# Adding the softmax sums' small constant on ScalarE instead of VectorE, in a newly drawn order of all steps

## The chip, the core and the metric

The kernel runs on one core of one Trainium2 chip. The metric is device time in microseconds (us) of one execution of the whole program. In the profile PE is TensorE, PEld its weight loads, DVE is VectorE, ACT is ScalarE, POOL is GpSimd, and SP is the engine that issues all transfers here.

## The reference

```
scores = scale * np.matmul(q, k.transpose(0, 1, 3, 2))        # 4 batches, 8 heads, 768 tokens, 64 wide
keep = is_sink | in_window                                    # 4 sink tokens, window of 128
scores = np.where(keep, scores, -1000000000.0)
scores = scores - np.max(scores, axis=-1, keepdims=True)
a = np.exp(scores)
a = a / (np.sum(a, axis=-1, keepdims=True) + 1e-09)
x = np.matmul(a, v)                                           # heads side by side: 3072 x 512
...
h = x @ w_in                                                  # 3072 x 1024
e = np.exp(h - h_max)
sm = e / (np.sum(e, axis=-1, keepdims=True) + 1e-09)
solu = h * sm
ln = (solu - mu) / np.sqrt(var + 1e-06) * g_ln
return ln @ w_out                                             # 3072 x 512
```

The change concerns the `+ 1e-09` in the attention's softmax.

## The kernel before

The 3072 tokens are worked in 24 chunks of 128 (chunk n, six for each batch). Since only 128 earlier keys and four sinks count, a chunk's scores need its own keys, those of the chunk ahead of it and the sinks. They lie in `ring`, where keys of four chunks fit.

The steps of one chunk, by the engine that does them:

- PE writes the scores of a head into one of two PSUM banks, `bank` (L654, L656, L657).
- DVE chooses between the two key chunks (`pick`, L663), adds the mask and takes the row's extreme (`mask`, L674, out `sc` and `nmx`). This frees the bank for the next but one head.
- ACT takes the exponential of each head and sums it (`exps`, L685, out `sc` and `ssum`).
- For four heads at a time (a half of the chunk, `hb`), DVE adds the constant to the 128x4 sums (L690, out `rs`) and inverts the result (L691). Both lines are the step `invert`; there are 48 of them.
- POOL multiplies the probabilities by the inverse: L700 in place, or L704 into `pn` for the chunks that are transposed by way of DRAM (`pd`, `pb`, then DVE L725). The others are transposed on PE (L732).
- POOL masks the transposed probabilities `pt` into `pc` and `pt` (L741, L747), and PE multiplies them with the values (`av`, L795).
- ACT and DVE split the result into a high part `xh` (L800) and a low part `xl` (L804), and PE multiplies both by the first weights (`h`, L815, three matmuls for each of eight pieces).
- Then come the row's maximum (DVE L820), the exponential (ACT L825), the product (DVE L830), the centring (ACT L846), a transposition by way of DRAM (`ud`, `ub`, DVE L872), the split into `uh` (ACT L886) and `ul` (DVE L890), and the second weights on PE (`o`, L902). ACT scales the result (L908), and SP stores it (L913).

At the start the weights come in as 64-bit words. They are narrowed by ACT and DVE (`wraw`, `wps`, `wbits`, lines 421 to 464), while the first chunks are already on their way. POOL also makes the low part of the keys (L625).

Nothing chooses the order at run time. The table `ORDER` at the head of the file lists all 2679 steps (a step is a function, a chunk and a part), and the program issues them in that order; each engine works its own instructions in the order in which they stand there, and waits for what is not ready:

```
    for at in ORDER:
        f, n, i = steps[at]
        f(n, i)
```

Of the kernel before, what the change touches and what calls it, by code (L numbers as in the profile page):

```python
# [157 lines left out]
P = 128  # L158
# [58 lines left out]
def _banded(ctx, tc, q, k, v, n_sink, window, w_in, w_out, g_ln, out, val, wts, wpool, consts):  # L217
# [11 lines left out]
    HB = 4  # L229
# [458 lines left out]
    def invert(n, hb):  # L688
        rs = st["rs", n, hb] = sm.tile([P, HB], F32, tag="rs", name=f"rs_{n}_{hb}")
        nc.vector.tensor_scalar(rs, st["ssum", n, hb], EPS_SUM, None, op0=ALU.add)  # L690
        nc.vector.reciprocal(rs, rs)  # L691
# [226 lines left out]
    def kept(k):  # L918
        return lambda n: 0 if carried(n) else k
# [201 lines left out]
```

## Time and profile before

| what | us |
|---|---|
| three runs | 438.46, 440.33, 1389.28 |
| their median | 440.33 |
| span of the profiled execution, first to last instruction | 437.9 |
| fastest run less that span | 0.56 |

The profile gives no other time for the profiled execution than its span. Busy times add an engine's instructions over the span, and a chain follows the work that ended last back to the start, at each step to what released it. Matmuls overlap each other in the records, so that PE's busy time holds short waits too.

### The profile page before, as it was taken

What the parts mean: (1) busy time and instruction counts of PE and PEld (TensorE: products, weight loads), DVE (VectorE), ACT (ScalarE), POOL (GpSimd) and SP (SyncE); (2) the same over time, 40 slices, a digit from 0 to 9 for tenths busy, and PEclk for the clock granted to TensorE, in tenths of its full rate; (3) what the DMA queues carried; (4) which work ended last, traced back from release to release, by engine and by line L of the source; (5) the groups of instructions that cost most, each with busy time, mean ns of one, the idle gap of its engine ahead of it and who ended that gap; (6) DMA issues with size and microseconds to landing.
All of it is one profiled execution on the core that took longest, in us unless ns stands there. A gap on an engine that the chain in (4) does not pass through costs nothing.

```text
span 437.9 us, 8516 instructions
## 1 busy us (share of the span) xinstructions
PE 415.4 (95%) x2507; PEld 332.6 (76%) x2507; DVE 360.9 (82%) x1029; ACT 315.7 (72%) x817; POOL 234.2 (53%) x388
## 2 busy tenths in 40 slices
PE   4899999999999999999999999999999999999994
PEld 3447777878787888878777787878878778888884
DVE  2989999997999889999989997899899797674520
ACT  5989988978877776877768576768767675555551
POOL 7742626658867552788454736556623673624020
PEclk9999999999999999999999999999999999999999
DMA  8999449999899899976998989966966558623001
GB/s 225 324 284 293 96 101 168 180 151 196 218 161 216 208 185 253 195 229 190 180 239 210 207 219 226 193 173 179 269 176 216 170 165 227 188 96 121 24 26 55
DMA packets 164025, 81.38 MB, mean 186 GB/s; under 512 B 120188, under 2 KB 150788, under 8 KB 163972
## 3 DMA queue, kind: packets, MB, share of 16 engines
q1 hardware_dynamic: 163972, 80.77, 82.3%
q8 instruction: 22, 0.36, 0.4%
q14 instruction: 31, 0.25, 0.2%
HBM read 45.62 MB, written 23.72 MB: 158 GB/s over the span
## 4 chain that ended last, share of the span: by engine, by line
PE 53%; DVE 25%; DMA 6%; issue 5%; POOL 4%; ACT 4%; SPq 1%; DVEq 0%; POOLq 0%; ACTq 0%
PE o L902 18%; PE h L815 17%; PE av L795 5%; DVE qT L600 4%; DVE sc L674 3%; DVE bank L663 3%; PE bank L656 3%; PE bank L657 2%; PE ws L443 2%; DMA pb<-pd 2%; DVE ul L890 2%; DVE nm L820 2%; PE bank L654 2%; DMA wraw<-in_moe_w_in_dram 1%; DVE pt L725 1%
## 5 line engine op out<-in xcount | busy, mean ns | idle before, releaser
L685 ACT ACTIVATE sc<-sc,nmx 128x132 f32<-128x132 f32 (+1 forms) x192 | 75.9, 396 | 25.1 <-DVE nmx L674 24.1
L902 PE MATMUL o<-w2h,uh 128*128 128x512 f32 (+1 forms) x200 | 79.7, 398 | 0.0
L815 PE MATMUL h<-w1h,xh 128*128 128x512 f32 x192 | 77.0, 401 | 1.0 <-DVE u L830 0.9
L902 PE MATMUL o<-w2h,ul 128*128 128x512 f32 (+1 forms) x200 | 77.0, 385 | 0.5 <-DVE ul L890 0.5
L902 PE MATMUL o<-w2l,uh 128*128 128x512 f32 (+1 forms) x200 | 77.2, 386 | 0.0
L815 PE MATMUL h<-w1h,xl 128*128 128x512 f32 x192 | 75.9, 395 | 0.6 <-DVE xl L804 0.5
L815 PE MATMUL h<-w1l,xh 128*128 128x512 f32 x192 | 75.3, 392 | 0.0
L625 POOL TENSOR_TENSOR ring<-kf,ring 64x512 fp32r<-64x512 f32 x48 | 63.1, 1320 | 22.6 <-ACT ring L620 18.7
L674 DVE CUSTOM_DVE_ANT_0 sc<-bank,bias 128x132 f32<-128x132 f32 (+1 forms) x192 | 53.1, 288 | 9.4 <-PE bank L654 1.7
L704 POOL TENSOR_TENSOR pn<-sc,rs 128x512 f32<-128x512 f32 x26 | 28.0, 1079 | 53.1 <-DVE rs L691 19.2
L656 PE MATMUL bank<-ring,qT 128*128 128x264 f32 (+1 forms) x176 | 51.0, 300 | 1.9 <-DVE nmx L674 1.7
L657 PE MATMUL bank<-ring,qX 128*128 128x264 f32 (+1 forms) x176 | 48.3, 284 | 0.1
L700 POOL TENSOR_TENSOR sc<-sc,rs 128x528 f32<-128x528 f32 (+1 forms) x22 | 24.8, 1127 | 40.8 <-DVE rs L691 24.0
L902 PEld LDWEIGHTS o<-w2h,ul 128*128 128x128 f32 x200 | 37.5, 188 | 9.2 <-DVE ul L890 1.2
L902 PEld LDWEIGHTS o<-w2h,uh 128*128 128x128 f32 x200 | 37.6, 188 | 8.8 <-issue 3.1
L741 POOL TENSOR_SCALAR_AFFINE_SELECT pc<-pt 128x512 f32<-128x512 f32 x40 | 28.4, 716 | 29.4 <-DVE pt L725 25.5
L815 PEld LDWEIGHTS h<-w1h,xl 128*128 128x128 f32 x192 | 36.0, 188 | 10.6 <-DVE xl L804 2.8
L656 PEld LDWEIGHTS bank<-ring,qT 128*128 128x128 f32 x176 | 33.1, 188 | 12.0 <-DVE nmx L674 6.3
L815 PEld LDWEIGHTS h<-w1h,xh 128*128 128x128 f32 x192 | 36.1, 188 | 7.3 <-issue 0.8
L902 PEld LDWEIGHTS o<-w2l,uh 128*128 128x128 f32 x200 | 37.7, 188 | 5.0
L825 ACT ACTIVATE e<-h,nm 128x1024 f32<-128x1024 f32 x24 | 26.7, 1113 | 18.7 <-DVE nm L820 18.6
L815 PEld LDWEIGHTS h<-w1l,xh 128*128 128x128 f32 x192 | 36.2, 188 | 5.0
(146 smaller groups left out, 975.9 us busy)
## 6 DMA issues: line engine op xcount, KB each, us to landing
qX<-qT SPq DMA_DIRECT2D x88, 128.0 KB, 2.7
ud<-u SPq DMA_DIRECT2D x20, 512.0 KB, 4.3
ub<-ud SPq DMA_DIRECT2D x80, 128.0 KB, 3.5
pd<-pn SPq DMA_DIRECT2D x26, 256.0 KB, 3.0
pb<-pd SPq DMA_DIRECT2D x52, 128.0 KB, 3.4
vn<-in_v_dram SPq DMA_DIRECT2D x24, 256.0 KB, 4.3
out_dram<-ob SPq DMA_DIRECT2D x23, 256.0 KB, 2.6
kn<-in_k_dram SPq DMA_DIRECT2D x12, 384.0 KB, 6.6
```

What stands on the lines that cost most here:

```text
L625: nc.gpsimd.tensor_tensor(t[ROWS[1 - x]], src[ROWS[x]], t[ROWS[x]].bitcast(F32), op=ALU.subtract)
L656: nc.tensor.matmul(o, st["qT", n, x][:, r, :], rhs, start=True, stop=False)
L657: nc.tensor.matmul(o, st["qX", n, x][:, r, :], rhs, start=False, stop=True)
L674: nc.vector.tensor_tensor_reduce(out=st["sc", n, hb][:, j, c0:c1], in0=st["s", n, h].rearrange("p a x -> p (a x)")[:, c0:c1], in1=bias0 if ...
L685: nc.scalar.activation(sc[:, i, c0:c1], sc[:, i, c0:c1], AF.Exp, bias=nmx[:, i:i + 1], scale=-1.0, accum_out=ssum[:, i:i + 1])
L700: nc.gpsimd.tensor_tensor(sc[:, :, c0:c1], sc[:, :, c0:c1], rs.unsqueeze(2).to_broadcast([P, HB, c1 - c0]), op=ALU.mult)
L704: nc.gpsimd.tensor_tensor(pn.rearrange("p g h f -> p h g f"), sc[:, :, 4:SEG].rearrange("p h (g f) -> p h g f", f=32), rs.unsqueeze(2).uns ...
L741: nc.gpsimd.affine_select(pc, st["pt", n, hb], pattern=[[0, HB], [1, P]], compare_op=ALU.is_ge, fill=0.0, base=0, channel_multiplier=-1)
L795: nc.tensor.matmul(acc[ROWS[x], r, :], vals[:, 2 * r + x, :], p[:, 2 * jp + x, :], start=alone, stop=alone or (r, i) == (NPAIR - 1, 1))
L815: nc.tensor.matmul(st["h", n][:, cols], a[:, kt, :], w[:, kt, cols], start=(kt == 0 and m == 0), stop=(kt == KT1 - 1 and m == 2))
L825: nc.scalar.activation(e, st["h", n], AF.Exp, bias=st["nm", n], scale=1.0, accum_out=se)
L902: nc.tensor.matmul(st["o", n, i], a[:, kt % 4, :], part(w, kt)[:, i * wide:(i + 1) * wide], start=(kt == 0 and m == 0), stop=(kt == KT2 - ...
```

## The change

The step `invert` keeps the reciprocal on DVE. The addition becomes a step of its own, `floor_sum`, in which ACT copies the 128x4 sums and adds the constant on the way. With 48 more steps the numbers of all steps shift, and the table `ORDER` is another one, with all steps in an order that was made anew. The tiles, the buffers, the transfers and the arithmetic are the same.

```
 ORDER = (
-    346, 0, 143, 2, 144, 244, 60, 348, 351, 5, 6, 3, 69, 350, 7, 51, 8, 352, 24, 9, 147, 154, 345, 12, 42, 155, 353,
...
 )
...
+    def floor_sum(n, hb):
+        rs = st["rs", n, hb] = sm.tile([P, HB], F32, tag="rs", name=f"rs_{n}_{hb}")
+        nc.scalar.activation(rs, st["ssum", n, hb], AF.Copy, bias=EPS_SUM)
+
     def invert(n, hb):
-        rs = st["rs", n, hb] = sm.tile([P, HB], F32, tag="rs", name=f"rs_{n}_{hb}")
-        nc.vector.tensor_scalar(rs, st["ssum", n, hb], EPS_SUM, None, op0=ALU.add)
+        rs = st["rs", n, hb]
         nc.vector.reciprocal(rs, rs)
...
-        rest_k: 2, ring_sinks: 1, score: H, pick: H, mask: H, exps: NPAIR, invert: NHB, normalise: NHB, turn_p: kept(NHB),
+        rest_k: 2, ring_sinks: 1, score: H, pick: H, mask: H, exps: NPAIR, floor_sum: NHB, invert: NHB, normalise: NHB, turn_p: kept(NHB),
```

What this does to an engine's instructions is seen at two places. In the changed file line numbers are 3 higher down to `exps` and 6 higher behind `invert`.

**First place: DVE at the first half of chunk 11**, with the low part `xl` of chunk 9 close by. Before, DVE has the addition, the reciprocal and then `xl`:

```order
L663 COPY_PREDICATED bank_89<-m_prev,bank_89 128x128
L674 ISA sc_1_2492,nmx_1_2493<-bank_89,bias_114 128x132
L674 ISA nmx_1_2493 128x1
L690 TENSOR_SCALAR rs_0_2507<-ssum_0_2414 128x4
L691 RECIPROCAL rs_0_2507<-rs_0_2507 128x4
L804 TENSOR_TENSOR xl_2511<-av_2432,xh_2486 128x512
L663 COPY_PREDICATED bank_90<-m_prev,bank_90 128x128
```

Now DVE has `xl` ahead of the reciprocal, and no addition:

```order
L810 TENSOR_TENSOR xl_2498<-av_2442,xh_2477 128x512
L666 COPY_PREDICATED bank_89<-m_prev,bank_89 128x128
L677 ISA sc_1_2494,nmx_1_2495<-bank_89,bias_114 128x132
L677 ISA nmx_1_2495 128x1
L666 COPY_PREDICATED bank_90<-m_prev,bank_90 128x128
L697 RECIPROCAL rs_0_2485<-rs_0_2485 128x4
L878 STREAM_TRANSPOSE ur_0_2511<-ub_2428 128x512
```

The addition of that half has gone to ACT, where it stands behind the last two exponentials of its half:

```order
L806 CAST xh_2477<-av_2442 128x512
L623 CAST ring<-kf_2238 64x4x128
L762 CAST sk_2380<-sc_1_2306 128x4x8
L688 ACTIVATE sc_0_2394,ssum_0_2396<-sc_0_2394,nmx_0_2395 128x132 x2
L693 ACTIVATE rs_0_2485<-ssum_0_2396 128x4
L688 ACTIVATE sc_1_2494,ssum_1_2496<-sc_1_2494,nmx_1_2495 128x132 x2
L892 CAST uh_0_2534<-ur_0_2511 128x512
```

So one DVE instruction of the half is gone, one ACT instruction has come, and `xl` stands one reciprocal and one head's mask earlier on DVE.

**Second place: PE between the values (`av`) and the first weights (`h`) of chunk 4.** Before, two pieces of chunk 1's second weights (`o`) and two heads' scores of chunk 5 (`bank`) stand between them:

```order
L795 MATMUL av_1242<-pt_1_1193,vn_629 64x128 x2
L902 MATMUL o_0_1269<-w2h_658,uh_0_1170 128x512
L902 MATMUL o_0_1269<-w2l_659,uh_0_1170 128x512
L902 MATMUL o_0_1269<-w2h_658,ul_0_1207 128x512
...
L656 MATMUL bank_89<-ring,qT_1_982 128x264
L657 MATMUL bank_89<-ring,qX_1_1015 128x264
L815 MATMUL h_1296<-w1h,xh_1289 128x512
```

Now five pieces of the second weights, four heads' scores and one transposition stand there:

```order
L801 MATMUL av_1254<-pt_1_1217,vn_672 64x128 x2
L659 MATMUL bank_90<-ring,qT_1_1012 128x264
L660 MATMUL bank_90<-ring,qX_1_1019 128x264
...
L908 MATMUL o_0_1276<-w2h_770,uh_0_1153 128x512
L908 MATMUL o_0_1276<-w2l_771,uh_0_1153 128x512
L908 MATMUL o_0_1276<-w2h_770,ul_0_1235 128x512
...
L738 MATMUL ptp_0_1311<-ident,sc_0_1100 128x128 x4
L908 MATMUL o_0_1276<-w2h_1085,uh_1_1290 128x512
L908 MATMUL o_0_1276<-w2l_1086,uh_1_1290 128x512
L908 MATMUL o_0_1276<-w2h_1085,ul_1_1305 128x512
L821 MATMUL h_1327<-w1h,xh_1322 128x512
```

So the first weights of that chunk stand three pieces, two heads' scores and a transposition further behind the values whose split they need. PE's work as a whole is the same.

## Rows read from the trace of the kernel before

**Rows 1.** The page's first part: busy us, share of the span and number of instructions of each engine.

```profile
PE 415.4 (95%) x2507; PEld 332.6 (76%) x2507; DVE 360.9 (82%) x1029; ACT 315.7 (72%) x817; POOL 234.2 (53%) x388
```

**Rows 2.** The page's chain of work that ended last, as shares of the span, by engine.

```profile
PE 53%; DVE 25%; DMA 6%; issue 5%; POOL 4%; ACT 4%; SPq 1%; DVEq 0%; POOLq 0%; ACTq 0%
```

**Rows 3.** Busy time in three stages of the span: from and to, length, then for PE, PEld, DVE, ACT and POOL busy us (instructions), the granted clock, DMA share and GB/s.

```profile
0.00:100.00 100.00, 88.70 (x508) 66.16 (x509) 85.82 (x253) 85.63 (x214) 54.42 (x93) 1.00 0.92 202
100.00:400.00 300.00, 294.42 (x1802) 239.08 (x1801) 263.68 (x760) 214.35 (x577) 172.68 (x278) 1.00 0.89 199
400.00:437.90 37.90, 32.31 (x200) 27.39 (x198) 11.41 (x16) 15.75 (x27) 7.15 (x19) 0.99 0.11 36
```

**Rows 4.** The same columns for two slices within the first stage.

```profile
40.00:60.00 20.00, 18.51 (x129) 14.91 (x129) 19.61 (x58) 18.90 (x52) 10.51 (x13) 1.00 0.64 149
60.00:80.00 20.00, 18.71 (x134) 14.92 (x129) 19.51 (x55) 17.82 (x41) 10.89 (x14) 1.00 0.79 119
```

**Rows 5.** PE's timeline near 100 us: start, duration, engine, line, operation.

```profile
99.78 0.39 PE L902 MATMUL o<-w2h,uh 128*128 128x512 f32 x1
100.01 0.39 PE L902 MATMUL o<-w2l,uh 128*128 128x512 f32 x1
100.24 0.39 PE L902 MATMUL o<-w2h,ul 128*128 128x512 f32 x1
```

**Rows 6.** The groups of the addition and of the reciprocal: count, busy us, mean ns of one, idle us of DVE just before them and what ended it; then the shortest, median and longest of each.

```profile
L690 DVE TENSOR_SCALAR rs<-ssum 128x4 f32<-128x4 f32 x48 | 11.8, 246 | 2.8 <-ACT sc L685 2.8
L691 DVE RECIPROCAL rs<-rs 128x4 f32<-128x4 f32 x48 | 8.5, 178 | 1.6
L690 DVE TENSOR_SCALAR rs<-ssum x48: 126/166/1169, 20.1 to 398.9; 128x4 f32<-128x4 f32 x48
L691 DVE RECIPROCAL rs<-rs x48: 177/178/180, 20.3 to 399.1; 128x4 f32<-128x4 f32 x48
```

**Rows 7.** The additions (L690) alone, by stage: DVE busy us (count).

```profile
0.00:100.00 100.00, 1.75 (x11) 1.00 0.92 202
100.00:300.00 200.00, 7.61 (x25) 1.00 1.02 206
300.00:437.90 137.90, 2.44 (x12) 1.00 0.50 144
```

**Rows 8.** The timeline around the addition for the first half of chunk 11, DVE, POOL and PE in order of their starts.

```profile
184.00 2.54 POOL L625 TENSOR_TENSOR ring<-kf,ring 64x512 fp32r<-64x512 f32 x2
...
185.68 0.88 DVE L690 TENSOR_SCALAR rs<-ssum 128x4 f32<-128x4 f32 x1
...
186.60 0.18 DVE L691 RECIPROCAL rs<-rs 128x4 f32<-128x4 f32 x1
186.70 0.66 DVE L804 TENSOR_TENSOR xl<-av,xh 128x512 fp32r<-128x512 f32 x1
187.01 1.04 POOL L704 TENSOR_TENSOR pn<-sc,rs 128x512 f32<-128x512 f32 x1 [0.47 <-DVE rs L691]
...
187.41 0.19 PEld L815 LDWEIGHTS h<-w1h,xl 128*128 128x128 f32 x1 [0.90 <-DVE xl L804]
187.41 0.50 PE L815 MATMUL h<-w1h,xl 128*128 128x512 f32 x1 [0.46 <-DVE xl L804]
```

**Rows 9.** DVE's timeline around an addition that no POOL instruction overlaps.

```profile
43.99 0.16 DVE L690 TENSOR_SCALAR rs<-ssum 128x4 f32<-128x4 f32 x1
44.19 0.18 DVE L691 RECIPROCAL rs<-rs 128x4 f32<-128x4 f32 x1
44.46 1.23 DVE L820 TENSOR_REDUCE nm<-h 128x1 f32<-128x1024 f32 x1
```

**Rows 10.** The groups of ACT's smallest instructions (columns as in rows 6).

```profile
L756 ACT CAST sk<-sc 128x32 fp32r<-128x32 f32 x40 | 8.4, 212 | 13.9 <-POOL sc L708 9.6 <-POOL sc L700 4.2
L310 ACT COPY g_sb<-spread 128x8 f32<-128x8 f32 x1 | 0.2, 164 | 0.0
L308 ACT COPY val<-spread 128x2 f32<-128x2 f32 x1 | 0.2, 153 | 0.0
```

**Rows 11.** What PE and its weight loads waited for on DVE: engine, out, line and releaser, us in total, times, longest.

```profile
PE bank L656 <- DVE nmx L674: 1.7, 4, 0.8
PEld bank L656 <- DVE nmx L674: 6.3, 14, 1.2
PEld h L815 <- DVE xl L804: 2.8, 8, 0.9
```

**Rows 12.** What POOL waited for at its multiplications (columns as in rows 11).

```profile
POOL sc L700 <- DVE rs L691: 24.0, 13, 5.5
POOL pn L704 <- DVE rs L691: 19.2, 10, 6.8
```

**Rows 13.** The end of the timeline: PE's last matmul and ACT's last scaling.

```profile
432.03 0.28 PE L902 MATMUL o<-w2h,ul 128*128 128x256 f32 x1
432.39 0.47 ACT L908 ACTIVATE ob<-o,al 128x256 f32<-128x256 f32 x1 [1.56 <-PE o L902]
```

266 rows, old and new, of the table ORDER are left out of this document.

## The prediction

> **What bounds the kernel now.** I began with the busy times of the whole span. PE stands at 95%, DVE at 82%, ACT at 72% [rows 1], and a reader would stop at PE. The timeline says why not: a full matmul is 0.39 us long in the records and the next one starts 0.23 us after it [rows 5], so a wait of up to 0.16 us between two matmuls still counts as busy. The 95% hides many short waits. The chain is the better view: only 53% of the span goes through PE and 25% through DVE, but 4% each through ACT and POOL [rows 2]. So DVE is the second bound.
>
> By stage the picture changes. In the first 100 us, where the weights are narrowed, DVE (85.82) and ACT (85.63) are equally loaded and PE has 11.3 us of plain idle [rows 3]; between 40 and 60 us DVE has 0.4 us left of 20 and ACT 1.1 [rows 4]. From 100 to 400 us PE is at 294.42 of 300, DVE at 263.68 and ACT at 214.35 [rows 3]: here ACT has room (85.7 us idle), DVE little. Behind 400 us nothing of the change is left; PE ends its last projections, and ACT scales the last one at 432.39 [rows 13].
>
> Where DVE holds PE up is seen in the waits: PE's weight loads and matmuls waited 6.3 and 1.7 us for a score bank that DVE had not cleared, and the loads 2.8 us for the low part `xl` [rows 11].
>
> **What the change removes.** 48 additions, 11.8 us of DVE [rows 6]. The reciprocal behind each stood idle for another 1.6 us in all [rows 6], because it needs the addition's result: in a plain case the addition starts at 43.99 and the reciprocal at 44.19, 0.04 us after its end [rows 9]. So DVE's queue is shortened by 11.8 + 1.6 = 13.4 us, 0.28 us each. Of the 11.8 us, 48 x 0.166 (the median) = 8.0 are the instruction itself; the other 3.8 come from a few that take up to 1.169 us, while no reciprocal takes over 0.180 [rows 6]. One of the long ones runs 185.68 to 186.56 while POOL makes the low keys (184.00 to 186.54), and ends with it; behind it `xl` starts at 186.70, and PE's load stands 0.90 us [rows 8]. So the addition waits for POOL at times, and PE pays. 7.61 of the 11.8 us lie between 100 and 300 us [rows 7], the stage in which DVE's time is worth most. [...]
>
> **What it adds.** 48 ACT instructions. No row shows this one. The nearest from below is 0.153 us (a 128x2 copy), from above 0.212 us (a 128x32 cast that reads SBUF, as this does) [rows 10]: 7.3 to 10.2 us. I take 0.2 us, near the cast, 9.6 us in all. It stands behind its own half's exponentials, so it waits for nothing else.
>
> [...]
>
> The reciprocal now waits for ACT's sum where the addition waited before (2.8 us [rows 6]); exponentials, one ACT-to-DVE step, then POOL, as before. If ACT is late, what stands behind the reciprocal is late too: masks, hence score banks, hence PE. That is the price if the cover goes. POOL's waits for the inverse (24.0 and 19.2 us [rows 12]) are long, but POOL is busy at 53%, so they are not worth anything by themselves.
>
> **What the order moves.** The listings show two kinds: `xl` put ahead of the reciprocal, and more PE work between a chunk's values and its first weights. At chunk 4 this is three more pieces of three matmuls at 0.23 us [rows 5], some 2.1 us without the scores. That is longer than the longest wait for `xl` (0.9 us [rows 11]), so such waits should mostly go where the order does this. Elsewhere an order drawn anew can make waits that were not there. No row prices that. Its bound on either side is PE's plain idle between 100 and 400 us, 300 - 294.42 = 5.6 us [rows 3]: it can go, or as much can come.
>
> **The sum**, against the profiled span of 437.9 us. DVE's 13.4 us count with DVE's share of the chain, 25% [rows 2]: -3.4. The bounds are 0 (all of it beside PE's work) and -13.4 (DVE on the path at every one). ACT's 9.6 us count with 4%: +0.4; bounds 0 and +9.6. The order: half of the waits for `xl`, 2.8 / 2 = -1.4. Together 437.9 - 3.4 + 0.4 - 1.4 = 433.5 us. The fastest run lies 0.56 us above the span, so the time would be **434.0 us**, 1.4% under the median of 440.33 and 1.0% under the fastest run.
>
> **The rivals.**
>
> *Hidden anyway.* PE has its fixed work and DVE's relief only lengthens DVE's idle time. For it: PE's 294.42 of 300; against it: PE waits for DVE by name [rows 11]. Time: 437.9 + 0.4 + 0.56 = 438.9.
>
> *ScalarE becomes the bound in the first 100 us.* The place is ACT's queue between 40 and 80 us, where it has 1.1 + 2.2 = 3.3 us idle [rows 4] and DVE less. Eleven additions fall into the first 100 us [rows 7], 2.2 us. As long as they fit into ACT's gaps nothing happens; once a late one holds the exponentials or weight casts behind it, each costs its full length, and DVE's relief there (1.75 us) doesn't pay, since DVE then waits for ACT. If half of all 48 land on the path, 4.8 us: 437.9 + 4.8 + 0.56 = 443.3. With 5.6 us of new PE waits from the order, 448.9. [...]
>
> *More comes back than the chain says.* The long additions sit just ahead of what PE waits for [rows 8], so that half of 13.4 and all of the `xl` waits return: 437.9 - 6.7 - 2.8 + 0.4 + 0.56 = 429.4.
>
> That the change fails to free DVE is excluded: the reciprocal has a constant price [rows 6].
>
> **Chances.** The forecast 0.45, hidden anyway 0.25, ScalarE as the bound 0.18, more comes back 0.12. The range from 428 to 443 takes in the times of the fourth and the second and reaches almost to the third's; outside I leave 0.06 below and 0.12 above. About 2% is what a measurement of this kernel can tell from no change: 431.5 and 449.1 around 440.33. Faster than that is the fourth case and a little of the first, 0.15; slower is the far end of the third, 0.06; within 2% the rest, 0.79.
>
> **What would show it.** Right: DVE busy near 349 us, with no instruction over 0.2 us on `rs`; ACT near 325; the waits of PE for `xl` and for score banks under the 10.8 us of now; ACT's addition at 0.15 to 0.21 us. Wrong: the same waits with ACT or POOL named in place of DVE; the first 100 us longer, with ACT over 19 us of 20; or the additions on ACT well above 0.21 us each. The last stretch, from PE's last first-weight matmul to the end, should stay as it is.

## The result and the profile after

The changed kernel takes 427.29 us (median; 427.12 to 427.54). The kernel before beside it took 438.46, 440.33 and 442.59 us, and 1389.28 us in one run, which the ratio leaves out: 0.9712 with a 95% interval of 0.9671 to 0.9753. The change is 2.9% faster; the forecast was 1.4%, and 427.29 lies just under the range.

The page of the changed kernel begins with its busy times; the second line is the chain that ended last, by engine.

```profile
PE 409.9 (96%) x2507; PEld 334.0 (79%) x2507; DVE 338.7 (80%) x981; ACT 323.5 (76%) x865; POOL 231.8 (54%) x388
PE 81%; ACT 5%; DMA 5%; DVE 3%; issue 3%; SPq 2%; POOL 1%; DVEq 0%; POOLq 0%; ACTq 0%
```

DVE lost 22.2 us against [rows 1], not the 11.8 us of the additions, and its share of the chain fell from 25% to 3% [rows 2]. The stages of the changed kernel, columns as in [rows 3], and then the two slices of [rows 4]:

```profile
0.00:100.00 100.00, 89.52 (x518) 67.73 (x519) 83.80 (x251) 89.62 (x237) 55.19 (x94) 1.00 0.94 202
100.00:400.00 300.00, 299.61 (x1872) 248.50 (x1871) 248.72 (x722) 224.96 (x615) 174.61 (x288) 1.00 0.88 200
400.00:425.50 25.50, 20.77 (x120) 17.81 (x118) 6.18 (x9) 8.95 (x16) 1.99 (x6) 0.98 0.12 44
...
40.00:60.00 20.00, 18.89 (x129) 15.32 (x129) 18.72 (x51) 19.20 (x54) 11.01 (x15) 1.00 0.76 172
60.00:80.00 20.00, 18.79 (x137) 15.13 (x134) 17.23 (x51) 18.73 (x46) 11.70 (x13) 1.00 0.73 122
```

PE's plain idle time between 100 and 400 us fell from 5.58 to 0.39 us, and it issued 1872 matmuls there instead of 1802. The first 100 us are no shorter: the low part `xl` of chunk 4 starts at 98.2 us, before at 96.6. From there the lead builds up, with steps back, to 13.6 us at the `xl` of chunk 23 (394.0 against 407.6). The rest takes 31.5 us after it, 30.3 before; the last two rows of the next listing are its end, as in [rows 13].

The new addition (L693) and the reciprocal (L697) as groups and as shortest, median and longest [rows 6]; then the waits of [rows 11] and [rows 12]:

```profile
L693 ACT ACTIVATE rs<-ssum 128x4 f32<-128x4 f32 x48 | 9.7, 204 | 0.9
L697 DVE RECIPROCAL rs<-rs 128x4 f32<-128x4 f32 x48 | 7.9, 166 | 3.2 <-ACT rs L693 2.8
L693 ACT ACTIVATE rs<-ssum x48: 188/205/208, 17.1 to 384.3; 128x4 f32<-128x4 f32 x48
L697 DVE RECIPROCAL rs<-rs x48: 134/170/179, 19.8 to 384.5; 128x4 f32<-128x4 f32 x48
...
PE bank L659 <- DVE nmx L677: 0.4, 2, 0.3
PEld bank L659 <- DVE nmx L677: 4.2, 14, 0.7
PEld h L821 <- DVE xl L810: 1.6, 5, 0.4
POOL pn L710 <- DVE rs L697: 39.2, 13, 7.0
POOL sc L706 <- DVE rs L697: 31.8, 14, 8.5
...
420.49 0.28 PE L908 MATMUL o<-w2h,ul 128*128 128x256 f32 x1
420.86 0.47 ACT L914 ACTIVATE ob<-o,al 128x256 f32<-128x256 f32 x1 [2.26 <-PE o L908]
```

PE's waits for score banks and `xl` went from 10.8 to 6.2 us. POOL waits longer for the inverse than before (71.0 against 43.2 us), in a kernel that got faster. Where did DVE's other 10.4 us go? The rest of q (before L600, now L603) tells: the same 34 instructions with both operands in SBUF, then the 10 that read PSUM, before and after.

```profile
L600 DVE TENSOR_TENSOR qT<-qf,qT 64x512 fp32r<-64x512 f32 x34 | 30.5, 898 | 2.3 <-ACT qT L592 1.3
L600 DVE TENSOR_TENSOR qT<-bank,qT 64x512 fp32r<-64x512 f32 x10 | 6.9, 689 | 2.2 <-ACT qT L592 1.9
```

```profile
L603 DVE TENSOR_TENSOR qT<-qf,qT 64x512 fp32r<-64x512 f32 x34 | 25.3, 745 | 3.3 <-ACT qT L595 2.1
L603 DVE TENSOR_TENSOR qT<-bank,qT 64x512 fp32r<-64x512 f32 x10 | 6.9, 688 | 4.1 <-ACT qT L595 3.9
```

The new order alone does that (740 ns in the run below that has it with the addition on DVE). The timeline of the kernel before shows how such a one gets long (two places, POOL and DVE):

```profile
135.93 1.27 POOL L625 TENSOR_TENSOR ring<-kf,ring 64x512 fp32r<-64x512 f32 x1 [0.27 <-POOL sk L763]
136.14 1.61 DVE L600 TENSOR_TENSOR qT<-qf,qT 64x512 fp32r<-64x512 f32 x1
...
200.50 1.29 POOL L625 TENSOR_TENSOR ring<-kf,ring 64x512 fp32r<-64x512 f32 x1
200.56 1.78 DVE L600 TENSOR_TENSOR qT<-qf,qT 64x512 fp32r<-64x512 f32 x1
```

DVE starts while POOL is at work, and ends 0.55 us after POOL's end, as if it had done little until then. The same collision that lengthened some additions [rows 8] lengthened bigger instructions too, these two to 1.61 and 1.78 us from a usual 0.684.

Two sums are used below. **Stalls**: for each two matmuls in a row, the time from start to start, less the lower quartile of that time for the same two lines; those over 0.15 us, from 100 us to 35 us before PE's last. Before: 9.42 us in 20 stalls; after: 0.72 in 2. **Collisions**: for DVE's rests of q and u, the weights' steps and the instructions on `rs`, the time above the usual one (0.684, 0.652, 0.68 to 0.70, 0.166 us), where it is over 0.1 us and POOL is at work. Before: 16.8 us in 33; after: 2.75 in 8.

### The profile page after: what moved, and what is told of

It is laid out like the page before. It is cut to its first block, busy times and chain, and to the rows that moved or that the text cites. A ratio compares the mean times of both kernels' runs of the same rounds, so it can differ in the third digit from the quotient of the medians.

```text
span 425.5 us, 8510 instructions
## 1 busy us (share of the span) xinstructions
PE 409.9 (96%) x2507; PEld 334.0 (79%) x2507; DVE 338.7 (80%) x981; ACT 323.5 (76%) x865; POOL 231.8 (54%) x388
## 4 chain that ended last, share of the span: by engine, by line
PE 81%; ACT 5%; DMA 5%; DVE 3%; issue 3%; SPq 2%; POOL 1%; DVEq 0%; POOLq 0%; ACTq 0%
PE o L908 28%; PE h L821 28%; PE av L801 8%; PE bank L659 5%; PE bank L660 4%; PE ptp L738 2%; DMA wraw<-in_moe_w_in_dram 2%; PE ws L446 1%; PE bank L657 1%; DMA kn<-in_k_dram 1%; DMA pb<-pd 1%; DVE qT L603 1%; PE av L790 1%; ACT wps L424 1%; DMA pd<-pn 1%
## 5 line engine op out<-in xcount | busy, mean ns | idle before, releaser
L659 PEld LDWEIGHTS bank<-ring,qT 128*128 128x128 f32 x176 | 33.1, 188 | 11.8 <-DVE nmx L677 4.2
L747 POOL TENSOR_SCALAR_AFFINE_SELECT pc<-pt 128x512 f32<-128x512 f32 x40 | 26.7, 672 | 25.1 <-DVE pt L731 18.1
```

Of the source, the lines that this page charges most:

```text
L659: nc.tensor.matmul(o, st["qT", n, x][:, r, :], rhs, start=True, stop=False)
L747: nc.gpsimd.affine_select(pc, st["pt", n, hb], pattern=[[0, HB], [1, P]], compare_op=ALU.is_ge, fill=0.0, base=0, channel_multiplier=-1)
```

## The experiments

Theory A: DVE's relief, the 48 additions gone, makes the gain. Theory B: the new order makes it. Theory C: each gives a part. A table of all runs is at the end of the section.

**The new order, the addition back on DVE.**

```diff
 def floor_sum(n, hb):
-    rs = st["rs", n, hb] = sm.tile(...)
-    nc.scalar.activation(rs, st["ssum", n, hb], AF.Copy, bias=EPS_SUM)
+    pass
 def invert(n, hb):
+    rs = st["rs", n, hb] = sm.tile(...)
+    nc.vector.tensor_scalar(rs, st["ssum", n, hb], EPS_SUM, None, op0=ALU.add)
     nc.vector.reciprocal(rs, rs)
```

> The new order of steps, the addition back on VectorE, in the step that takes the reciprocal, as before the change. Theory A, VectorE's relief made the gain and the order little: 438 to 442 us. Theory B, the order made it (more other work between a producer and TensorE's need of it): 427 to 430 us, with VectorE's busy time up by about 10 us and TensorE's plain idle time from 100 to 400 us still under 1 us. Theory C, each gives a part: 431 to 437 us.

430.17 us, ratio 0.9785 (0.9752 to 0.9818), between the ranges of B and C. **The old order, the addition on ACT**, `floor_sum` put into the old `ORDER` right behind the later of the two `exps` steps of its half:

```diff
 exps(n, 2 * hb), ... exps(n, 2 * hb + 1),
+floor_sum(n, hb),
```

> The order of before, with the addition on ScalarE issued right behind the last exponential of its four heads, and nothing else moved. Theory A (relief): 427 to 431 us. Theory B (order): 438 to 442 us, with VectorE's busy time down by about 10 us all the same and TensorE's plain idle time from 100 to 400 us still above 4 us. Theory C: 432 to 437 us.

436.80 us, ratio 0.9926 (0.9898 to 0.9954), in the range of C. The two parts multiply to 0.9785 x 0.9926 = 0.9713, the whole change being 0.9712: theory C, with three quarters of it the order's. The new order with the addition on DVE, its busy line, its chain, and its slice and stage from 40 and from 100 us:

```profile
PE 412.4 (96%) x2507; PEld 333.7 (78%) x2507; DVE 350.2 (82%) x1029; ACT 315.9 (74%) x817; POOL 230.3 (54%) x388
PE 78%; DVE 7%; ACT 4%; DMA 4%; issue 3%; SPq 1%; POOL 1%; DVEq 0%; ACTq 0%
40.00:60.00 20.00, 19.53 (x129) 15.71 (x129) 19.10 (x56) 19.15 (x53) 11.34 (x15) 1.00 0.63 148
100.00:400.00 300.00, 298.14 (x1857) 245.32 (x1856) 256.75 (x762) 217.80 (x578) 174.22 (x289) 1.00 0.88 200
```

DVE does all the work of before and is 10.7 us shorter; the stalls are at 3.10 us, the collisions at 8.4. Of the 8.6 us by which the profiled span is shorter (429.3 against 437.9), 6.3 are fewer stalls. In the old order DVE got less out of the move: with the addition on ACT it is busy 8.8 us less than before (352.1 against 360.9) and not 11.8, in part since the rest of u got longer (a mean of 817 ns against 772), by my reading beside POOL as in the kernel before. The first line is that group before, the second and third are from the old order with the addition on ACT:

```profile
L890 DVE TENSOR_TENSOR ul<-ur,uh 128x512 fp32r<-128x512 f32 x40 | 30.6, 772 | 3.1 <-ACT uh L886 2.9
L904 DVE TENSOR_TENSOR ul<-ur,uh 128x512 fp32r<-128x512 f32 x40 | 32.4, 817 | 3.8 <-ACT uh L900 3.6
L705 DVE RECIPROCAL rs<-rs 128x4 f32<-128x4 f32 x48 | 8.2, 172 | 5.2 <-ACT rs L701 4.7
```

**The addition left out, in the old order and in the new one** (`floor_sum` does nothing):

```diff
 def invert(n, hb):
-    nc.vector.tensor_scalar(rs, st["ssum", n, hb], EPS_SUM, None, op0=ALU.add)
-    nc.vector.reciprocal(rs, rs)
+    nc.vector.reciprocal(rs, st["ssum", n, hb])
```

> The order of before with the addition of 1e-9 left out on every engine: the reciprocal reads the sums. VectorE is relieved and ScalarE gets nothing. Theory A (relief): 425 to 430 us, and a little under the run that adds on ScalarE. Theory B (order): 437 to 441 us. My forecast's own term for the relief (a quarter of 13.4 us) would give about 438 us here, from 441.5.

> The new order with the addition of 1e-9 left out on every engine: ScalarE is spared 48 instructions and 9.7 us of busy time against the changed kernel. If ScalarE's additions lie beside other work, 426.5 to 427.5 us, the same as the changed kernel. If ScalarE's chain share of 5% is what they cost, 426.8; if they stand on the path in full, 418 to 420 us.

434.89 us, ratio 0.9899 (0.9865 to 0.9933), and 426.42 us, ratio 0.9699 (0.9663 to 0.9734). So ACT's 48 additions cost 0.6 us in the new order (0.9712 to 0.9699) and 1.2 in the old one (0.9926 to 0.9899), with intervals that overlap: little or nothing of their 9.7 us. The last is the fastest kernel of the study, by a margin that these intervals don't settle. By the reference's formula the sum always contains exp(0) = 1, of which 1e-9 is a billionth.

**Halves of the order**, the addition on DVE: old up to the `x_lo` step of chunk 13 and then new, and the reverse.

```diff
-ORDER = old
+ORDER = old[:i + 1] + [s for s in new if s not in old[:i + 1]]
```

> Addition on VectorE; the order of before up to the step that makes xl of chunk 13 (250 us), and the new order behind it. In the traces the new order with the addition on VectorE is 3.7 us ahead at that step and 9.3 us at the last xl. If the order's gain is a sum of places, this keeps the later part, 5.6 us: 433.5 to 436 us, ratio 0.987. If a gain needs the whole order: 438 to 441 us.

> Addition on VectorE; the new order up to the step that makes xl of chunk 13, and the order of before behind it. If the order's gain is a sum of places, this keeps the earlier part, 3.7 us: 435 to 438 us, ratio 0.9915, and with the run of old order then new order the two gains add to about 9.5 us. If the later half of the old order takes an earlier lead back: 438.5 to 441 us.

437.67 us, ratio 0.9956 (0.9936 to 0.9975), and 433.95 us, ratio 0.9865 (0.9832 to 0.9898). Together 0.9822, a little less than the order's 0.9785 but within the intervals: a sum of places fits, and that some 1.6 us needs the whole order is not ruled out. Nothing is lost later: with the new order first, the lead at `xl` was 5.4 us at chunk 13 and 5.4 at chunk 23. I had the halves the wrong way round: the part up to 250 us carries more. The 3.7 us that I had read at chunk 13 came from one trace; the same steps, in this run's trace, were 5.4 us ahead, so a lead read from a single trace can be off by nearly 2 us.

**The new order at the old load**: the addition on DVE twice.

```diff
     nc.vector.tensor_scalar(rs, st["ssum", n, hb], EPS_SUM, None, op0=ALU.add)
+    nc.vector.tensor_scalar(rs, st["ssum", n, hb], EPS_SUM, None, op0=ALU.add)
     nc.vector.reciprocal(rs, rs)
```

> The new order with the addition on VectorE made twice into the same tile (the second writes what the first wrote): VectorE gets about 11 to 13 us more than in the new order with one addition (430.2 us), which itself has 11.5 us more than the changed kernel (427.3). If a microsecond of VectorE costs the same everywhere (2.9 us for 11.5), 433 to 433.5 us. If the new order has cover for it, under 432; if VectorE becomes the bound, over 437.

435.77 us, ratio 0.9907 (0.9874 to 0.9940): more than the 433 to 433.5 us of a constant price, less than the 437 us of a DVE that is the bound. Its two groups of additions, its busy line and its chain:

```profile
L696 DVE TENSOR_SCALAR rs<-ssum 128x4 f32<-128x4 f32 x48 | 14.2, 296 | 0.9 <-ACT sc L688 0.9
L697 DVE TENSOR_SCALAR rs<-ssum 128x4 f32<-128x4 f32 x48 | 9.3, 194 | 1.6
...
PE 413.9 (95%) x2507; PEld 333.0 (77%) x2507; DVE 360.6 (83%) x1077; ACT 315.9 (73%) x817; POOL 228.9 (53%) x388
PE 66%; DVE 17%; ACT 5%; issue 5%; DMA 4%; POOL 2%; SPq 1%; DVEq 0%; ACTq 0%; POOLq 0%
```

By chance DVE is now as busy as before (360.6 and 360.9 us). So at the same DVE time the new order is still 0.93% or 4.1 us better, and 10.4 us of DVE cost 5.4 us (0.9907 less 0.9785, of 440). In the old order 10.2 us less brought 4.4 us (the run without the addition), in the new one 12.9 us less brought 3.8 (0.9785 to 0.9699).

**Can the old order be mended by hand?** First PE's cover: 16 steps pulled ahead of stalled ones, such as

```diff
-value(10), project(7, 3), ... score(8, 5), ... project(3, 5)
+project(7, 3), value(10), ... project(3, 5), score(8, 5), ...
```

> The kernel before, addition on VectorE as it was, with one edit to the order: in the trace of before TensorE starts 20 times between 100 and 400 us over 0.15 us later than usual for that pair of matmuls, 9.42 us together. Ahead of 16 of these steps (7.16 us) one project or hidden step of TensorE is pulled forward whose inputs were ready at that moment by the trace; no other engine's order changes. Theory cover (the order's gain is TensorE finding other work in these moments): 432.5 to 435.5 us, a ratio of about 0.985, with VectorE's busy time still near 360 us. Rival, collisions (the order's gain is VectorE's 10.7 us shorter busy time beside GpSimd): VectorE's busy time is unchanged here, so 438 to 441 us. Rival, the stall moves to the next step: 438 to 441 us with as many stalls elsewhere.

438.80 us, ratio 0.9984 (0.9962 to 1.0005), stalls 7.52 us in 20. Theory cover falls. Both rivals had forecast this time; that there are again 20 stalls speaks for the one in which the stall moves. Then DVE's collisions, by pulling ready DVE steps ahead of instructions that collided:

```diff
-rest_q(13, 0), ... turn_q(14, 0), ... flip_p(11, 0)
+turn_q(14, 0), flip_p(11, 0), rest_q(13, 0), ...
```

> The kernel before, addition on VectorE as it was, with one edit to the order: in its trace 33 VectorE instructions that read and write SBUF (the q rest, the u rest, the addition, a few of the weights) run over their usual time while GpSimd is at work, 16.8 us together. Ahead of 23 of them, 13.3 us of it, one to three VectorE steps are pulled forward that were ready by the trace and are not lengthened beside GpSimd; no other engine's order changes. Theory collisions (part of the new order's gain is that VectorE runs clear of GpSimd): VectorE's busy time falls from 361 to 348 to 354 us and, at 0.5 us for each (5.6 us for 10.4 between one addition and two in the new order), the time to 434 to 437 us, ratio 0.987 to 0.992. Rival, the collisions only move to the next instruction: VectorE stays at 358 to 361 us and the time at 438.5 to 441. Rival, VectorE is shorter but what it was pulled ahead of is late: busy time falls, the time does not.

446.63 us, ratio 1.0134 (1.0084 to 1.0184), though DVE fell to 353.7 us and collisions to 7.7. I had not asked whether a pulled transpose's transfer had landed. DVE's timeline there, and the matmul that PE starts next:

```profile
203.78 0.71 DVE L733 STREAM_TRANSPOSE pt<-pb 128x512 f32<-128x512 f32 x1 [1.55 <-DMA pb<-pd]
204.52 1.48 DVE L608 TENSOR_TENSOR qT<-qf,qT 64x512 fp32r<-64x512 f32 x1
206.38 0.47 PE L664 MATMUL bank<-ring,qT 128*128 128x128 f32 x1 [2.53 <-DVE nmx L682]
```

The masks behind it were late, and PE stood 2.7 us, as it did for 3.1 us before 297, behind a second transpose that waited 1.20 us for its transfer. The wait for the transfer is only a part of each hole: both times a long rest of q, 1.48 and 1.53 us for its usual 0.684, stood behind the transpose, while POOL was busy 1.74 us of 205 to 207 and 2.81 us of 294 to 297. The same kind of pull was made at four places of the new order without the addition:

> The new order without the addition of 1e-9 on any engine (426.4 us), and with the same kind of pull at 4 of the 5 places where VectorE still runs over its time beside GpSimd, 1.7 us of it. TensorE's stalls over 0.15 us between 100 and 400 us are down to 0.99 us there, so there is little left to win: 425.5 to 426.5 us. If collisions still cost half of their length: 425.6.

432.23 us, ratio 0.9823 (0.9778 to 0.9868), 1.3% worse than the order it started from, with one stall of 3.1 us: DVE stood 2.86 us before a pulled transpose of u (the trace names no releaser), and `xl` was behind it.

```profile
197.54 0.71 DVE L885 STREAM_TRANSPOSE ur<-ub 128x512 f32<-128x512 f32 x1 [2.86 <-issue]
199.74 0.50 PE L828 MATMUL h<-w1h,xl 128*128 128x512 f32 x1 [2.92 <-DVE xl L817]
```

The old order again, with pulls only of steps that wait for no transfer:

```diff
-rest_q(13, 0), ... turn_q(14, 0), ... rest_q(13, 1), ... turn_k(16, 0)
+turn_q(14, 0), rest_q(13, 0), ... turn_k(16, 0), rest_q(13, 1), ...
```

> The run with VectorE's steps pulled forward, mended: there two of the pulled steps waited for a transfer (1.55 us at 203 us) and TensorE behind them for 2.7 and 3.1 us, after the first of which the granted clock was 0.50 for some 6 us. Now only steps are pulled that wait for no transfer and whose buffer was free by the trace: 19 of 26 places, 10.5 us of lengthened VectorE time; addition on VectorE, the other engines' orders as before. Theory collisions (VectorE's time beside GpSimd costs about half of its length): VectorE's busy time 351 to 355 us, no stall of TensorE over 1 us, 435 to 437.5 us, ratio 0.989 to 0.995. Rival, the steps that are jumped over are needed as early as they stood: busy time falls the same, the time stays at 438.5 to 441 us, with new waits of TensorE for the score banks.

438.31 us, ratio 0.9951 (0.9933 to 0.9969), between the two forecasts. DVE at 353.9 us, collisions 8.2 us, stalls 9.24. So 7.0 us less of DVE's time brought 2.2 us, 0.31 for each. That is the net of what the pulls brought and what they cost: against the forecast there is a stall over 1 us, and a pull made it. The maximum of chunk 18 (L828) was put ahead of a rest of u, which then ended no earlier than before (at 341.49; before 341.50, last line), though PE was there sooner:

```profile
339.49 1.22 DVE L828 TENSOR_REDUCE nm<-h 128x1 f32<-128x1024 f32 x1
340.62 0.87 DVE L898 TENSOR_TENSOR ul<-ur,uh 128x512 fp32r<-128x512 f32 x1
341.55 0.49 PE L910 MATMUL o<-w2h,ul 128*128 128x512 f32 x1 [1.11 <-DVE ul L898]
...
340.23 1.27 DVE L890 TENSOR_TENSOR ul<-ur,uh 128x512 fp32r<-128x512 f32 x1
```

The lead over the kernel before was 2.1 us at the `xl` of chunk 16 and 0.9 at that of chunk 23. At last both repairs, PE's pulls planned anew:

```diff
+project(7, 3), value(10), ... turn_q(14, 0), rest_q(13, 0), ...
```

> Both hand repairs of the order of before together, addition on VectorE: VectorE's steps pulled forward as in the run before this one (0.9951), and, by that run's own trace, one ready project or hidden step of TensorE pulled ahead of 15 of the 18 steps that it starts over 0.18 us late (6.3 of 9.1 us). If the two repairs only add, 0.9951 times 0.9984: ratio 0.9935, 436 to 438 us. If TensorE's pulls failed alone because VectorE stayed late, and VectorE's failed to reach TensorE because its cover was short, together they give more: 432.5 to 435 us, ratio 0.983 to 0.989, towards the new order with the addition on VectorE (0.9785). If neither carries, 438.5 to 440.

438.94 us, ratio 0.9961 (0.9939 to 0.9982), in the range of "neither carries". The gain is no larger than that of the product of the two, 0.9935: nothing shows that the repairs help each other.

All runs, by order, where the addition is, DVE's busy time, stalls, collisions and ratio:

```text
order            addition    DVE us  stalls us (n)  collisions us (n)  ratio
old              DVE         360.9    9.42 (20)     16.8 (33)          1
old              ACT         352.1    6.70 (17)     13.1 (25)          0.9926
old              none        350.7    5.10 (12)     12.6 (26)          0.9899
new              DVE twice   360.6    5.31 (12)     11.9 (25)          0.9907
new              DVE         350.2    3.10 (7)       8.4 (19)          0.9785
new              ACT         338.7    0.72 (2)       2.8 (8)           0.9712
new              none        337.3    0.99 (2)       2.8 (9)           0.9699
old, then new    DVE         355.8    7.27 (15)     13.6 (29)          0.9956
new, then old    DVE         355.8    4.95 (11)     12.6 (25)          0.9865
old, PE pulled   DVE         360.3    7.52 (20)     15.6 (31)          0.9984
old, DVE pulled  DVE         353.7   17.28 (33)      7.7 (18)          1.0134
old, DVE ready   DVE         353.9    9.24 (19)      8.2 (20)          0.9951
old, both        DVE         354.6    7.27 (20)      9.7 (22)          0.9961
new, DVE pulled  none        338.0    4.19 (3)       2.7 (7)           0.9823
```

## Why the prediction was right or wrong

**DVE's relief and ACT's price: right in their sum, by luck in the terms.** The steps -3.4 and +0.4 make -3.0 us; the old order with the addition on ACT measured 0.9926, -3.3 us. Taken singly, leaving the addition out brought 4.4 us for my 3.4, and ACT's addition took 1.2 of it back for my 0.4, a difference within the noise. The 13.4 us of relief were too many: with the addition on ACT in the old order DVE was busy 8.8 us less, and the reciprocal stood 5.2 us idle where addition and reciprocal together had stood 4.4 [rows 6]. The chain's share was right by luck too: it was 25% where 10.2 us brought 4.4 us, and 7% in the new order, where 12.9 us brought 3.8. It tells who is waited for now, and it is no price. ACT's instruction took 204 ns for my 200, and ACT's busy time came to 323.5 us for 325.

**The order: the step that failed.** I put it at -1.4 us with a bound of 5.6 either way; it measured -9.5 us (0.9785). The waits for `xl` did go from 2.8 to 1.6 us in the changed kernel, as I had it, but the new order alone took 6.3 us of stalls from PE and 10.7 us of busy time from DVE. Two faults made the bound too small. I took PE's plain idle time as all that an order could win, after I had written that waits of up to 0.16 us between matmuls count as busy. By starts instead of ends, the same trace held 9.42 us of stalls. And I held DVE's time to be fixed but for the additions. I had one collision on record [rows 8] and read it as a feature of the addition; 16.8 us of them lay in the trace, most of it on the rests of q (7.1 us) and u (3.8 us). The forecast "DVE near 349 us" missed 10.7 us for that.

**What the order's 9.5 us are.** Shown: they are there without moving the addition; both halves give a part; at equal DVE time 4.1 us are left. The other 5.4 us go with DVE's 10.4 us, by the run that gives DVE that time back as small additions. Each of the two figures is good to some 1.5 to 2 us. That a collision costs the same as an addition was only argued: taken out by hand in the old order, 7.0 us brought 2.2 us. What in the order gives the 4.1 us stays open; in the traces the stalls are less by as much (9.42 to 5.31 us), which says where the time lies and not why. More work between a DVE result and PE's use of it was my reading, and pulling single steps of PE brought 0.16%, with an interval that holds zero. The new order also moves the steps of ACT, POOL and SP, which every repair by hand left as they were, and no run moved those alone. An order in which everything is placed together does what these local repairs don't; which feature does it, no run isolates.

**The rivals.** Hidden anyway (438.9 us) falls: relief alone has intervals below 1 in both forms. ScalarE as the bound (443 to 449 us) falls, although both signs that I had named for it came: ACT is busy 19.20 of 20 us between 40 and 60, and the `xl` of chunk 4 is 1.6 us later. Both belong to the new order and not to ACT's additions: with the addition on DVE, ACT is busy 19.15 of 20 us there, and that `xl` starts at 99.3, later still. Leaving ACT's additions out brings about 1.2 us or less. "More comes back" (429.4 us) came nearest in time with the wrong sum: it took 6.7 us for relief and 2.8 for `xl`, measured were 3.3 for the move and 9.5 for the order.

**Around the span** I added 0.56 us, the fastest run less the profiled span. The two were not the same execution: in the runs made beside the experiments, where both are on record for each execution, the kernel before takes 1.97 to 2.15 us more than its span. With that the same sum gives about 435.5 us, so the forecast was some 1.5 us too low by it, which here brought it nearer to the result: luck again.

## What to carry to other kernels

Where an order is drawn anew beside an edit, run the edit in the old order and the new order without the edit; the larger part may be the one that the description doesn't name. Look for an engine's own instructions that take longer than their shortest twin, and what other engine was at work then: DVE's time for the same work was 360.9 us in the old order and 350.2 in the new one. When a step is moved ahead by hand, ask for its transfers and buffers too, since PE stood 2.7 and 3.1 us behind two late steps, and the repairs at nineteen places brought 2.2 us.

## What was not expected of the hardware

**DVE beside POOL.** The rest of q grew only where both inputs lie in SBUF (a mean of 898 ns, against 689 where one lies in PSUM). The transposes of u, from SBUF with one input, did not (702 ns in the old order, 698 in the new one). In the kernel before 12 of the 34 rests of q with both inputs in SBUF took over 0.1 us more than usual: each started 0.02 to 1.16 us after a POOL instruction that was still at work, and ended 0.54 or 0.55 us after it. The other way round there is the same: POOL's low keys take 1.27 to 1.35 us, but in four of 48 cases 1.63 to 1.82, and in each of the four a DVE instruction with two SBUF inputs was already under way, such as

```profile
50.93 0.68 DVE L435 SCALAR_TENSOR_TENSOR wbits<-wraw,wbits 128x512 int32<-128x512 int32 x1
50.95 1.82 POOL L625 TENSOR_TENSOR ring<-kf,ring 64x512 fp32r<-64x512 f32 x1
```

One input alone is no safeguard, though: the 128x4 addition has one, and took 0.88 us beside POOL for its usual 0.166 [rows 6], [rows 8]. What makes an instruction long there, no run shows.

**At one hole in PE's work the granted clock fell to 0.50.** In the run with DVE's steps pulled forward PE stood 2.7 us before 206.4. Its windows behind that (columns as in [rows 3]), then its timeline:

```profile
205.00:207.00 2.00, 0.62 (x3) 0.62 (x4) 1.97 (x6) 0.64 (x3) 1.74 (x4) 0.76 0.00 0
207.00:209.00 2.00, 2.00 (x7) 1.71 (x7) 1.90 (x9) 2.00 (x8) 1.85 (x4) 0.50 0.00 0
209.00:211.00 2.00, 2.00 (x6) 1.52 (x6) 1.20 (x2) 0.14 (x2) 1.41 (x3) 0.50 1.02 301
211.00:213.00 2.00, 2.00 (x7) 1.54 (x6) 0.00 (x0) 0.00 (x0) 0.08 (x1) 0.53 1.02 245
213.00:215.00 2.00, 2.00 (x11) 1.60 (x10) 1.35 (x4) 0.42 (x2) 0.00 (x0) 1.00 1.16 229
...
294.00:297.00 3.00, 0.48 (x2) 0.44 (x3) 2.94 (x4) 0.58 (x4) 2.81 (x3) 1.00 0.26 58
297.00:300.00 3.00, 3.00 (x17) 2.50 (x16) 2.94 (x6) 0.00 (x0) 2.19 (x3) 1.00 0.00 0
```

```profile
208.25 0.63 PE L823 MATMUL h<-w1h,xl 128*128 128x512 f32 x1
208.68 0.63 PE L823 MATMUL h<-w1h,xh 128*128 128x512 f32 x1
209.11 0.63 PE L823 MATMUL h<-w1l,xh 128*128 128x512 f32 x1
```

The granted clock is 0.50 to 0.53 for some 6 us, and matmuls start 0.43 us apart instead of 0.23 [rows 5]: about 3 us more, an estimate from the two spacings. After the hole at 294 to 297 us it stays at 1.00; of the three holes over 2 us that the kept traces have behind 100 us, this one alone has the lower clock. That the hole brought it down is not shown. The times of the four pulls in the new order fit: the profiled execution, its hole of 3.1 us with the clock at 1.00 behind it, took 429.52 us at a mean clock of 0.999; the other five took 431.6 to 432.7 at 0.992 to 0.996. That their clock fell behind the same hole is not shown, since no trace of them is kept, and a mean of 0.996 alone says nothing: the kernel before has it in a quarter of its runs, which are no slower than the others.
